# Loading q and k six tokens a partition and turning them by DMA from there, for batches 2 to 7 of an attention and MLP kernel

## The chip, the cores and the metric

The kernel runs on one core of one Trainium2 chip. The metric is the device time of one execution in microseconds; given is the median of the runs.

## What is computed

Attention with a forget gate, for 8 batches of 8 heads, 576 tokens and 64 channels a head; then an MLP over the 4,608 tokens:

```python
scores = q @ k.T / sqrt(64);  cum = cumsum(log(clip(f, 0.0001, 1)))
scores = where(causal, -1e9, scores + cum[i] - cum[j])
attn = softmax(scores);  x = attn @ v            # x: 4608 x 512, heads side by side
h = x @ w_in                                     # 512 x 2048
out = (h - tanh(h)) @ w_out                      # 2048 x 512
```

## The kernel before

**Stages.** The work goes by pairs of heads: pair p is heads 2c and 2c+1 of batch b, with p = 4b + c, so four pairs a batch and 32 in all. The loop at the end takes one pair after another; a pair's stage has seven score tiles, `ti` = 0 to 6 (`scores`). Between the tiles the loop writes, in an order fixed by hand, what else belongs to the stage: the product with v of the pair before (`values`), its division on VectorE, the turn of that result into `XR`, the MLP's input (`turn`, from batch 1 on by DMA from SP's queue), and some 6 to 8 pieces of the MLP (`mlp1`, `mlp2_plain`, `mlp2`), whose number `TAKE` sets. The MLP goes by units of 512 tokens. Every engine executes in the order of this program and waits on semaphores.

**Banks.** A score tile goes to one of two PSUM banks (`ps_sc`). The MLP takes three banks (`ps_m`) by turns and, after `widen(1)`, the bank `ps_tr` too.

**q and k.** A score matmul contracts over channels, so it needs q and k turned: channel on the partition, token along the row, in `QT` and `KT` (two buffers each, for even and odd batches), below them three rows for the decay. There are two ways to that form:

- Batches 0 to 2. `load_qk` brings a batch's heads to `qn`, `kn` with six neighbouring tokens on each of 96 partitions. `trans` turns one pair on TensorE by six transposes (two tokens by 64 channels, from 96 partitions, each), into a PSUM bank, and two copies take that to `QT` or `KT`, even tokens by one and odd tokens by the other. For batch 2 this is done in the stages of pairs 7 and 8, two pairs in each; one copy of the two is on VectorE and the other, put off by `LATER` and `rest`, on ScalarE. In these stages `keep` takes one of the three MLP banks out of turn for it; `widen(1)` comes in pair 9's stage.
- Batches 3 to 7 (`FAR` = 3). `load_block` brings 128 tokens, one a partition, in five loads for q and five for k. `turn_block` turns each block on SP's queue by a DMA transpose into `TQ` (two buffers) or `TK` (one), with two heads on the 128 partitions and the tokens in order. `place` then copies from there: k by four copies of two heads on VectorE, q by four copies of one head on ScalarE and two of two heads on VectorE.

The dictionary `LOADS` says at which pair and tile a load, a turn or a copy is written into the program; `add` fills it, batch by batch. With p0 = 4(b - 1), the first pair of the batch before, k of batch b is placed in the stages p0 + 3 and p0 + 4, its q on ScalarE in stage p0 and on VectorE in stage p0 + 1 (for batch 3 three stages later).

Of the kernel before, what the change touches and what calls it, by code (L numbers as in the profile page):

```python
# [21 lines left out]
def kernel(  # L22
# [44 lines left out]
    ps_m = ctx.enter_context(tc.tile_pool(name="ps_m", bufs=1, space=PSUM))  # L67
    M_AT, KEPT = [0], []

    def m_bank(name):  # L70
        while M_AT[0] % 3 in KEPT:
            M_AT[0] += 1
        M_AT[0] += 1
        return ps_m.tile([P, 512], FP32, tag=f"m{(M_AT[0] - 1) % 3}", name=name)

    def keep():
        while M_AT[0] % 3 in KEPT:
            M_AT[0] += 1
        KEPT.append(M_AT[0] % 3)

# [12 lines left out]
    qn, kn = ([t[0:S // NT6, :].rearrange("p (h n d) -> p h n d", h=H, n=NT6) for t in raw] for raw in (qraw, kraw))  # L93
    qb, kb = ([t[:, 0:NJ * DM].rearrange("p (n e) -> p n e", n=NJ) for t in raw] for raw in (qraw, kraw))
    vn = [qkp.tile([P, NJ, H, VW], FP16, tag=f"vn{i}", name=f"vn{i}") for i in range(2)]
# [9 lines left out]

    def load_block(dst, src, b, n):
        pn = min(P, S - n * P)
        nc.gpsimd.dma_start(out=dst[b % 2][0:pn, n, :].rearrange("p (h d) -> p h d", h=H),  # L108
                            in_=src[b, :, n * P:n * P + pn, :].rearrange("h p d -> p h d"))

    def turn_block(dst, src, b, n):
        pn = min(P, S - n * P)
        nc.sync.dma_start_transpose(out=dst[:, :, n * P:n * P + pn], in_=src[b % 2][0:pn, n, :])

    def place(dst, src, b, a, c, n, eng):
        to, of = dst[b % 2][0:D, 2 * c + a:2 * c + a + 2 * n - 1:2, 0:S], src[a * D:(a + 1) * D, c:c + n, :]
        if eng == "A":
            nc.scalar.activation(out=to, in_=of, func=AF.Copy)
        else:
            (nc.gpsimd if eng == "P" else nc.vector).tensor_copy(out=to, in_=of)  # L120

# [120 lines left out]
    for b in range(2, B):  # L242
        p0 = (b - 1) * NPAIR
        at_q = [(p0 - 2, n + 2) for n in range(NJ)]
        at_k = [(p0, n) for n in range(NJ)]
        at_v = [(p0 + (1 if b >= FAR else 2), n) for n in range(NJ)]
        to_q, to_k = (p0 - 1, 1), (p0 + 1, 4)
        on_q = p0
        on_k = (p0 + 3, 0), (p0 + 3, 2), (p0 + 4, 1), (p0 + 4, 4)
        if b == FAR:  # L250
            at_q = [(p0 - 1, n + 1) for n in range(NJ)]
            to_q, on_q = (p0, 4), p0 + 3
            on_k = (p0 + 3, 2), (p0 + 3, 4), (p0 + 4, 0), (p0 + 4, 4)
        add((p0, 0), load_aug, b)
        for n in range(NJ):
            if n < NJ - 1:
                add(at_v[n], load_v_block, b, n, 0, H)
            else:
                add(at_v[n], load_v_rest, b)
            if b < FAR:  # L260
                continue
            add(at_q[n], load_block, qb, q, b, n)
            add(at_k[n], load_block, kb, k, b, n)
            add(to_q, turn_block, TQ[b % 2], qb, b, n)
            add(to_k, turn_block, TK, kb, b, n)
        if b < FAR:
# [3 lines left out]
        for n, (c, a) in enumerate(((0, 0), (0, 1), (2, 0), (2, 1))):  # L270
            add(on_k[n], place, KT, TK, b, a, c, 2, "V")
            add((on_q, (1 if b == FAR else 3) + n), place, QT, TQ[b % 2], b, a, c // 2, 1, "A")
            if c:
                add((on_q + 1, 1 + 2 * a), place, QT, TQ[b % 2], b, a, c, 2, "V")

# [11 lines left out]
    def trans(b, c, src, dst, early, copies, split=False):  # L287
        pn, g3 = S // NT6, NT6 // 2
        if early:
            t32 = m_bank("t32")  # L290
        elif KEPT and src is kn:
            t32 = ps_m.tile([P, UW], FP32, tag=f"m{KEPT[0]}", name="t32")
        else:
            t32 = ps_tr.tile([P, UW], FP32, tag="tr", name="t32")
# [296 lines left out]
    def att_items(p):  # L591
# [8 lines left out]
        for ti in range(len(TILES)):  # L600
# [12 lines left out]
            if ti == 5 and p < NPAIR - 1:  # L613
                put(trans, *pairs[p + 2], qn, QT, True, "VV")
            if p in (2 * NPAIR - 1, 2 * NPAIR, 2 * NPAIR + 1) and (ti % 2 or ti == 0):
# [42 lines left out]
    for p in range(len(pairs) + 1):  # L658
# [17 lines left out]
        for emit, counts in items:  # L676
            emit()
            n += counts
            while n > first and given < len(mine) and given * (whole - first) < (n - first) * len(mine):
                fn, *args = mine[given]  # L680
                fn(*args)
                given += 1
    widen(2)
    for fn, *args in mlp[at:]:
# [29 lines left out]
```

## Time and profile before

| | before |
|---|---|
| median of 3 runs | 338.77 us (338.75 to 339.58) |
| profiled execution, span of its instructions | 337.1 us |
| its own time over the span | within 1.7 us, by the median of the runs |
| TensorE busy | 330.0 us (98%) |
| VectorE busy | 260.8 us (77%) |
| ScalarE busy | 233.2 us (69%) |
| GpSimd busy | 163.2 us (48%) |
| DMA packets | 147,468, of which 128,181 under 512 B |

In the rows of a profile PE is TensorE, PEld its weight loads, DVE VectorE, ACT ScalarE, POOL GpSimd, and SPq the queue of DMAs that SyncE issues. "L311 DVE COPY KT<-t 64x576 f16<-64x576 f16 x16 | 12.8, 799 | ..." is a group: line, engine, operation, written tile and read tile, shapes, count, busy time in us, mean duration in ns, and then the idle time before it. A row of the timeline begins with its start and its duration in us.

### The profile page before, as it was taken

The numbers are of one execution on the slowest core, as the hardware profiler recorded it, in microseconds if no ns is written. First come the engines' busy times: TensorE is split into PE (matmuls) and PEld (weight loads), VectorE is DVE, ScalarE is ACT, GpSimd is POOL, SyncE is SP. The second block draws the span as 40 slices with busy tenths as digits, with TensorE's granted clock in tenths as the row PEclk, the third lists the DMA queues.
The fourth block names the chain that finished last, engine by engine and source line by source line (L and its number), as shares of the span: only waits on it lengthen the run. The fifth ranks groups of instructions, "written<-read, shape, count | busy, mean of one in ns | idle before, by whom it ended". The sixth has DMA issues, their size and how long they took to land.

```text
span 337.1 us, 8726 instructions
## 1 busy us (share of the span) xinstructions
PE 330.0 (98%) x3313; PEld 235.6 (70%) x3313; DVE 260.8 (77%) x509; ACT 233.2 (69%) x438; POOL 163.2 (48%) x321
## 2 busy tenths in 40 slices
PE   8899999999999999999999999999999999999996
PEld 8775558875687558845888888656865686486485
DVE  7998986659887886778867896788668866966865
ACT  6997777978977886788677867787558733632630
POOL 8977467775667564767377637722322210000000
PEclk9999999999999999999999999999999999999999
DMA  9999999999979997999899999990130022002003
GB/s 113 143 203 202 186 198 165 184 159 172 142 87 190 136 134 72 164 152 139 94 122 187 118 112 117 163 132 18 51 113 2 19 65 97 2 31 95 0 12 116
DMA packets 147468, 38.82 MB, mean 115 GB/s; under 512 B 128181, under 2 KB 146335, under 8 KB 147426
## 3 DMA queue, kind: packets, MB, share of 16 engines
q0 software_dynamic: 94528, 18.37, 75.5%
q1 hardware_dynamic: 52892, 19.89, 32.4%
q8 instruction: 26, 0.43, 0.6%
q14 instruction: 16, 0.13, 0.2%
q10 hardware_dynamic: 6, 0.01, 0.0%
HBM read 36.85 MB, written 9.44 MB: 137 GB/s over the span
## 4 chain that ended last, share of the span: by engine, by line
PE 90%; DVE 7%; ACT 2%; issue 1%; ACTq 0%
PE hps L451 36%; PE ops L517 29%; PE ps L352 11%; PE av L389 8%; PE ops L492 4%; DVE KT L311 2%; DVE QT L311 1%; PE t L298 1%; ACT e L361 1%; DVE xn L400 1%; DVE gq L462 0%; DVE TQ L187 0%; ACT th L456 0%; PE x L417 0%; DVE clo L190 0%
## 5 line engine op out<-in xcount | busy, mean ns | idle before, releaser
L451 PE MATMUL hps<-XR,win 128*128 128x512 f16 (+1 forms) x640 | 140.7, 357 | 0.3 <-DVE gq L462 0.3
L456 ACT ACTIVATE th<-hps 128x512 f32<-128x512 f32 x144 | 86.6, 602 | 55.5 <-PE hps L451 53.5
L361 ACT ACTIVATE e<-ps 128x512 f16<-128x512 f32 x192 | 110.2, 597 | 8.9 <-PE ps L352 7.4
L462 DVE TENSOR_TENSOR gq<-hps,th 128x512 f16<-128x512 f32 x144 | 98.0, 687 | 23.6 <-ACT th L456 22.0
L371 POOL TENSOR_SCALAR_AFFINE_SELECT e<-e 128x128 f16<-128x128 f16 x168 | 60.7, 364 | 71.5 <-ACT e L361 68.7
L451 PEld LDWEIGHTS <-win 128*128 128x128 f16 x640 | 57.7, 97 | 49.0 <-issue 1.1
L352 PE MATMUL ps<-QT,KT 67*128 67x64 f16 (+4 forms) x384 | 76.5, 276 | 2.0 <-DVE KT L311 1.4
L517 PEld LDWEIGHTS <-gq 128*128 128x128 f16 x640 | 60.3, 97 | 11.1
L517 PE MATMUL ops<-wout,gq 128*128 128x256 f16 x512 | 63.2, 272 | 0.0
L352 PEld LDWEIGHTS <-KT 67*128 67x128 f16 x384 | 36.4, 98 | 23.4 <-DVE KT L311 2.0
L389 PEld LDWEIGHTS <-e 128*128 128x128 f16 x896 | 32.3, 97 | 3.6
L389 PE MATMUL av<-vn,e 128*128 128x65 f16 x896 | 33.6, 193 | 0.0
L517 PE MATMUL ops<-W,sq 128*128 128x256 f16 x256 | 31.2, 272 | 0.0
L131 POOL DMA_DIRECT2D vn<-in_v_dram x32 | 28.0, 877 | 6.5 <-DMA win<-in_moe_w_in_dram 2.9
L400 DVE TENSOR_TENSOR xn<-av,rs 128x640 f16<-128x640 f32 x32 | 26.4, 825 | 1.3 <-DVE rs L399 0.2
L517 PEld LDWEIGHTS <-sq 128*128 128x128 f16 x256 | 24.1, 97 | 3.4
L108 POOL DMA_DIRECT2D kn<-in_k_dram x25 | 21.2, 848 | 2.1 <-issue 1.8
L108 POOL DMA_DIRECT2D qn<-in_q_dram x25 | 21.2, 848 | 1.8 <-issue 1.4
L371 POOL TENSOR_SCALAR_AFFINE_SELECT el<-el 128x128 f16<-128x128 f16 x28 | 9.3, 333 | 26.1 <-ACT el L361 25.8
L398 DVE TENSOR_SCALAR rs<-av 128x10 f32<-128x10 f32 x32 | 5.2, 163 | 18.2 <-PE av L389 17.0
L532 ACT ACTIVATE m<-ops 128x512 f32<-128x512 f32 x16 | 9.5, 596 | 10.9 <-PE ops L517 10.9
L484 DVE TENSOR_TENSOR gq<-gq 128x512 f16<-128x512 f16 x32 | 17.1, 533 | 0.0
(83 smaller groups left out, 311.8 us busy)
## 6 DMA issues: line engine op xcount, KB each, us to landing
out_dram<-ost SPq DMA_DIRECT2D x34, 256.0 KB
vn<-in_v_dram POOLq DMA_DIRECT2D x24, 128.0 KB, 6.2
qn<-in_q_dram POOLq DMA_DIRECT2D x20, 128.0 KB, 5.0
kn<-in_k_dram POOLq DMA_DIRECT2D x20, 128.0 KB, 5.6
win<-in_moe_w_in_dram POOLq DMA_DIRECT2D x2, 1024.0 KB, 11.8
wout<-in_moe_w_out_dram POOLq DMA_DIRECT2D x2, 1024.0 KB, 15.6
XR<-xn SPq DMA_TRANSPOSE x56
qn<-in_q_dram POOLq DMA_DIRECT2D x6, 144.0 KB, 4.6
```

The lines of the kernel that those rows point to most:

```text
L108: nc.gpsimd.dma_start(out=dst[b % 2][0:pn, n, :].rearrange("p (h d) -> p h d", h=H), in_=src[b, :, n * P:n * P + pn, :].rearrange("h p d - ...
L131: nc.gpsimd.dma_start(out=vn[b % 2][:, n, h0:h1, 0:D], in_=v[b, h0:h1, n * P:(n + 1) * P, :].rearrange("h p d -> p h d"))
L352: nc.tensor.matmul(out=ps[:, col:col + n], lhsT=kt[0:rows, h, j * P:(j + 1) * P], rhs=qt[0:rows, h, i0:i0 + n], start=True, stop=cut == 0)
L361: nc.scalar.activation(out=e[:, lo:hi], in_=ps[:, lo:hi], func=AF.Exp, bias=-SHIFT, scale=qscale)
L371: nc.gpsimd.affine_select(out=view, in_=view, compare_op=ALU.is_ge, fill=0.0, base=0, pattern=pat, channel_multiplier=-1)
L389: nc.tensor.matmul(out=av[:, a, ib, :], lhsT=E.pop((b, c, a, j, ib)), rhs=vn[b % 2][:, j, 2 * c + a, 0:D + 1], start=(j == 0), stop=(j == ib))
L400: nc.vector.tensor_tensor(out=xn.rearrange("p i (a d) -> p a i d", a=2), in0=av[:, :, :, 0:D], in1=rs.to_broadcast([P, 2, NJ, D]), op=ALU. ...
L451: nc.tensor.matmul(out=hps[:, o:o + n], lhsT=win[:, ci, ft * P:(ft + 1) * P], rhs=XR[:, ci, t:t + n], start=(ci == 0), stop=(ci == NCH - 1))
L456: nc.scalar.activation(out=th, in_=hps, func=AF.Tanh, scale=-1.0)
L462: nc.vector.tensor_tensor(out=GQ[(u, i)][:, half, kt, :], in0=hps, in1=th, op=ALU.add)
L484: nc.vector.tensor_tensor(out=LHS[name](u, i)[:, ks], in0=LHS[x](u, i)[:, ks], in1=LHS[y](u, i)[:, ks], op=op)
L517: nc.tensor.matmul(out=ps[:, m, :], lhsT=LHS[lhs](u, kt // 4)[:, kt % 4, m * P:(m + 1) * P], rhs=rhs[:, kt, :], start=(fresh and (apart or ...
```

## The change

q and k of batches 3 to 7 are loaded by `load_qk`, as those of batches 0 to 2 were: one DMA with six tokens a partition in place of five. `turn_raw` turns four heads of such a buffer by one DMA transpose, so two for q and two for k: 12 blocks of 128 by 96, each with two tokens by 64 channels on its partitions and one row of 96 token groups. So `TQ` and `TK` now hold, for a head, three such blocks, and even tokens lie on partitions 0 to 63, odd ones on 64 to 127. `place` copies one parity of four heads (on ScalarE of two): it reads tokens at a step of 96 elements and writes them at a step of 2.

Batch 2 goes this way too. Its loads stay in pair 4's stage; it is turned in pair 6's stage and placed by eight copies on VectorE in those of pairs 7 and 8. TensorE's transposes for it, their copies and `keep` are gone, and `widen(1)` comes in pair 7's stage. v of batch 2 is loaded in pair 7's stage in place of pair 6's. For batch 3, q is loaded, turned and placed in other stages than before; for batches 4 to 7 the loads stand at one tile.

```diff
-    def load_block(dst, src, b, n):
-    ...
-    def turn_block(dst, src, b, n):
-        pn = min(P, S - n * P)
-        nc.sync.dma_start_transpose(out=dst[:, :, n * P:n * P + pn], in_=src[b % 2][0:pn, n, :])
-
-    def place(dst, src, b, a, c, n, eng):
-        to, of = dst[b % 2][0:D, 2 * c + a:2 * c + a + 2 * n - 1:2, 0:S], src[a * D:(a + 1) * D, c:c + n, :]
+    def blocks(t):
+        return t.rearrange("p c (g r) -> p (c g) r", r=S // NT6)
+
+    def turn_raw(dst, src, b, h0, h1):
+        nc.sync.dma_start_transpose(out=blocks(dst)[:, 3 * h0:3 * h1, :],
+                                    in_=src[b % 2][0:S // NT6, h0 * NT6 * D:h1 * NT6 * D])
+
+    def place(dst, src, b, h0, h1, e, eng):
+        to = dst[b % 2][0:D, h0:h1, e:S:2].rearrange("d h (r g) -> d h r g", g=NT6 // 2)
+        of = blocks(src)[e * D:(e + 1) * D, 3 * h0:3 * h1, :].rearrange("d (h g) r -> d h r g", g=NT6 // 2)
...
     for b in range(2, B):
         p0 = (b - 1) * NPAIR
-        at_v = [(p0 + (1 if b >= FAR else 2), n) for n in range(NJ)]
+        late_b = b >= FAR
+        at_v = [(p0 + (1 if late_b else 3), n) for n in range(NJ)]
...
+        if not late_b:
             add((p0, 2), load_qk, qn, q, b, 0, H)
             add((p0, 5), load_qk, kn, k, b, 0, H)
+            for n in range(2):
+                add((p0 + 2, 1 + 3 * n), turn_raw, TQ[0], qraw, b, 4 * n, 4 * n + 4)
+                add((p0 + 2, 2 + 3 * n), turn_raw, TK, kraw, b, 4 * n, 4 * n + 4)
+                for e in range(2):
+                    add((p0 + 3 + n, 1 + e), place, QT, TQ[0], b, 4 * n, 4 * n + 4, e, "V")
+                    add((p0 + 3 + n, 4 + e), place, KT, TK, b, 4 * n, 4 * n + 4, e, "V")
             continue
...
+        at_q, at_k, to_q, to_k = (p0 - 2, 2), (p0, 1), (p0 - 1, 1), (p0 + 1, 4)
+        on_q = p0
+        on_k = (p0 + 3, 0), (p0 + 3, 2), (p0 + 4, 1), (p0 + 4, 4)
+        if b == FAR:
+            at_q, at_k, to_q, to_k = (p0, 1), (p0, 5), (p0 + 1, 4), (p0 + 2, 4)
+            on_q = p0 + 3
+            on_k = (p0 + 3, 2), (p0 + 3, 4), (p0 + 4, 0), (p0 + 4, 4)
+        add(at_q, load_qk, qn, q, b, 0, H)
+        add(at_k, load_qk, kn, k, b, 0, H)
+        for n in range(2):
+            add(to_q, turn_raw, TQ[b % 2], qraw, b, 4 * n, 4 * n + 4)
+            add(to_k, turn_raw, TK, kraw, b, 4 * n, 4 * n + 4)
+        for n in range(4):
+            m, e = divmod(n, 2)
+            add(on_k[n], place, KT, TK, b, 4 * m, 4 * m + 4, e, "V")
+            add((on_q, (1 if b == FAR else 3) + n), place, QT, TQ[b % 2], b, 2 * m, 2 * m + 2, e, "A")
+            if m:
+                add((on_q + 1, 1 + 2 * e), place, QT, TQ[b % 2], b, 4, H, e, "V")
...
-            if p in (2 * NPAIR - 1, 2 * NPAIR) and ti % 2 == 0:
-                pair = pairs[2 * NPAIR + 2 * (p - 2 * NPAIR + 1) + ti // 4]
-                put(trans, *pair, *((kn, KT) if ti % 4 else (qn, QT)), False, "VA")
...
         if p == 2 * NPAIR - 1:
-            keep()
-        if p == 2 * NPAIR + 1:
-            KEPT.clear()
             widen(1)
```

The order in which SP issues its DMAs in the stages of pairs 6 and 7. Before (XR is the turned result of a pair, out_dram an output of the MLP):

```order
L423 DMA_TRANSPOSE XR<-xn 128x4x128
L425 DMA_TRANSPOSE XR<-xn 128x64
L423 DMA_TRANSPOSE XR<-xn 128x4x128
L425 DMA_TRANSPOSE XR<-xn 128x64
L499 DMA out_dram<-ost 128x2x256
L423 DMA_TRANSPOSE XR<-xn 128x4x128
L425 DMA_TRANSPOSE XR<-xn 128x64
L499 DMA out_dram<-ost 128x2x256
```

The same place now:

```order
L417 DMA_TRANSPOSE XR<-xn 128x4x128
L419 DMA_TRANSPOSE XR<-xn 128x64
L102 DMA_TRANSPOSE TQ_107<-qn_97 128x12x96
L102 DMA_TRANSPOSE TK<-kn_99 128x12x96
L417 DMA_TRANSPOSE XR<-xn 128x4x128
L419 DMA_TRANSPOSE XR<-xn 128x64
L102 DMA_TRANSPOSE TQ_107<-qn_97 128x12x96
L102 DMA_TRANSPOSE TK<-kn_99 128x12x96
L493 DMA out_dram<-ost 128x2x256
L417 DMA_TRANSPOSE XR<-xn 128x4x128
L419 DMA_TRANSPOSE XR<-xn 128x64
```

Two turns of batch 2 stand ahead of the turns of pair 5's result, and two more behind them.

VectorE in the stages of pairs 7 and 8 (t is a bank with TensorE's transposes, rs and xn are the division of a pair's result, W a difference of output weights). Before:

```order
L462 TENSOR_TENSOR gq<-hps,th 128x512 x2
L311 COPY QT_103<-t_1152 64x576
L311 COPY KT_105<-t_1183 64x2x288
L398 TENSOR_SCALAR rs<-av 128x10
L399 RECIPROCAL rs<-rs 128x10
L400 TENSOR_TENSOR xn<-av,rs 128x2x5x64
L311 COPY QT_103<-t_1270 64x576
L311 COPY KT_105<-t_1300 64x2x288
L311 COPY QT_103<-t_1329 64x576
L278 TENSOR_TENSOR W_93<-wout 128x1024
L311 COPY KT_105<-t_1362 64x2x288
```

Now:

```order
L456 TENSOR_TENSOR gq<-hps,th 128x512 x2
L111 COPY QT_103<-TQ_107 64x1152 x2
L392 TENSOR_SCALAR rs<-av 128x10
L393 RECIPROCAL rs<-rs 128x10
L394 TENSOR_TENSOR xn<-av,rs 128x2x5x64
L111 COPY KT_105<-TK 64x4x288 x2
L111 COPY QT_103<-TQ_107 64x1152
L274 TENSOR_TENSOR W_93<-wout 128x1024
L111 COPY QT_103<-TQ_107 64x1152
```

Each copy of a pair from PSUM has become half of a copy of two pairs from `TQ` or `TK`, and the copies of pairs 8 and 9 into KT stand ahead of those of pairs 10 and 11 into QT. In the later stages the copies `place` stand where they stood, with another pattern.

More of the change, by code (lines that the diff above doesn't have):

```diff
@@ L67 @@
     ps_m = ctx.enter_context(tc.tile_pool(name="ps_m", bufs=1, space=PSUM))
-    M_AT, KEPT = [0], []
+    M_AT = [0]
     def m_bank(name):
-        while M_AT[0] % 3 in KEPT:
-            M_AT[0] += 1
         M_AT[0] += 1
         return ps_m.tile([P, 512], FP32, tag=f"m{(M_AT[0] - 1) % 3}", name=name)
[L76 to L79, printed above, removed]
     win = wpl.tile([P, NCH, DFF], FP16)
@@ L119, in place @@
         else:
-            (nc.gpsimd if eng == "P" else nc.vector).tensor_copy(out=to, in_=of)
+            nc.vector.tensor_copy(out=to, in_=of)
     def load_v_rest(b):
```

30 lines of the change are left out of this document (2 added, 28 removed).

## Prediction

> **What bounds the kernel now.** I read the page first, then its chain, then the busy time of each engine in the stages around the change, then single rows of the timeline, the groups by form and the DMA queues. A "stage" here is the stretch from the first score matmul of one pair of heads to the first of the next; stage 7 is pair 7's.
>
> ```profile
> span 337.1 us, 8726 instructions
> PE 330.0 (98%) x3313; PEld 235.6 (70%) x3313; DVE 260.8 (77%) x509; ACT 233.2 (69%) x438; POOL 163.2 (48%) x321
> PE 90%; DVE 7%; ACT 2%; issue 1%; ACTq 0%
> ```
>
> TensorE is busy for 98% of the span and holds 90% of the chain that ended last: its work sets the time. So a thing counts only if it takes matmuls off TensorE, or makes TensorE wait where it did not wait before.
>
> ```profile
> 50.75:59.31 8.56, 8.55 (x114) 7.47 (x114) 5.16 (x9) 6.44 (x11) 6.58 (x14) 1.00 2.04 163
> 86.50:95.00 8.50, 8.50 (x88) 6.08 (x87) 7.49 (x16) 8.40 (x17) 4.32 (x10) 1.00 1.90 131
> 95.00:103.40 8.40, 8.40 (x99) 7.21 (x98) 7.44 (x17) 5.96 (x12) 6.85 (x13) 1.00 0.94 100
> 148.14:156.50 8.36, 8.36 (x72) 4.49 (x70) 7.10 (x14) 7.03 (x15) 4.76 (x11) 1.00 1.84 141
> 156.50:165.74 9.24, 9.24 (x92) 6.44 (x90) 8.03 (x19) 6.52 (x14) 4.53 (x11) 1.00 1.26 116
> 165.74:174.16 8.42, 8.42 (x100) 7.22 (x99) 5.39 (x13) 6.08 (x12) 6.83 (x13) 1.00 0.92 93
> 174.16:183.55 9.39, 9.39 (x109) 8.02 (x107) 6.74 (x13) 6.86 (x14) 6.25 (x12) 1.00 1.81 185
> ```
>
> The rows are stages 7, 11, 12 and 18 to 21; after the length come PE, PEld, DVE, ACT and POOL, then the clock (1.00 throughout). TensorE fills every stage. VectorE has 8.03 of 9.24 us in stage 19 and leaves between 1.2 and 3.0 us in the stages around it; ScalarE has 8.40 of 8.50 us in stage 11.
>
> **Term 1: the turns of batch 2 leave TensorE.** Eight groups of six transposes (4 pairs, q and k) are in stages 7 and 8.
>
> ```profile
> 59.22 0.26 PE t L298 x6
> 59.47 0.22 PE ps L352
> L298 PE MATMUL t<-id,qn 96*128 96x96 f16 x72 | 5.0, 206 | 0.0
> ```
>
> The first two rows are of the chain in order of time: a group takes 0.26 us of TensorE's sequence. The third, 5.0 us for 72, would give 0.42 a group, but it counts the tail of the last transpose, under which the next matmul already runs. I take 8 x 0.26 = **2.1 us less**. Nothing else waits in its place by itself: TensorE had no idle time there to give back.
>
> **Term 2: what batch 2 now waits for.** q and k of batch 2 are loaded as before; now SP's queue must turn them once they land, and VectorE must place them before stage 8's first score. Before, TensorE turned them just ahead of use.
>
> ```profile
> qn<-in_q_dram POOLq DMA_DIRECT2D x1, 576.0 KB, 14.6
> kn<-in_k_dram POOLq DMA_DIRECT2D x1, 576.0 KB, 16.1
> 32.27 0.79 POOL L102 DMA_DIRECT2D qn<-in_q_dram  x1
> 33.80 0.78 POOL L102 DMA_DIRECT2D kn<-in_k_dram  x1
> 39.83 1.50 SPq L423 DMA_TRANSPOSE XR<-xn  x1
> 59.31 0.38 PE L352 MATMUL ps<-QT,KT 67*128 67x512 f16 x1
> ```
>
> q lands at 32.27 + 14.6 = 46.9, k at 33.80 + 16.1 = 49.9. Stage 8 begins at 59.31; four of the eight groups stand before it, so it would begin at 59.31 - 4 x 0.26 = 58.3. Between 46.9 and 58.3 must fit: the turn of q's first half, behind it in the same queue that of k's first half, and two copies on VectorE. How long a turn takes at that time is seen from the turn issued at 39.83, in the DMA rows of 40 to 43.5, 43.5 to 47.5 and 53 to 58 us:
>
> ```profile
> q0 software_dynamic: 1132, 0.69, 137.1%
> q8 instruction: 1, 0.02, 1.6%
> ...
> q0 software_dynamic: 834, 0.63, 100.2%
> q1 hardware_dynamic: 640, 0.15, 29.8%
> ...
> q0 software_dynamic: 3894, 0.61, 169.6%
> q1 hardware_dynamic: 591, 0.14, 30.2%
> ```
>
> Turns are in queue q1. None of its packets ran up to 43.5, some 4 us after the issue; then the 640 of one pair's turns took most of 4 us, beside the loads. Half of q (4 heads) is twice a pair's two heads, so 1,280 packets. At 640 in 4 us they would take 8 us; the load beside them is then the second half of the output weights, in smaller packets, that ends at about 53, so I take 5: 46.9 + 4 + 5 = 56. k's half follows at once, beside v's small packets, where both queues together pass (3894 + 591) / 5 = 900 packets a us; with half of that, 1280 / 450 = 2.8 us, it lands at 58.7. Two copies (0.79 each, below) end at 60.3, against 58.3: TensorE waits **2.0 us**. Bounds: if the 4 us to the first packet run while q's half is under way and k's half goes at 900 a us, it lands at 49.9 + 4 + 1.4 = 55.3, and there is no wait; at 8 us for q's half it lands at 61.7 and the wait is 5.0 us. I take the middle because the packets beside it are between those of the two rows. Behind the copies on VectorE stand the division of pair 6 and the differences of the weights, for which TensorE has a stage of time. On SP's queue pair 5's, 6's and 7's turns into XR now stand behind those of batch 2; pair 7's is wanted first for unit 1 of the MLP:
>
> ```profile
> 66.97 1.23 SPq L425 DMA_TRANSPOSE XR<-xn  x1
> 72.23 1.03 PE L451 MATMUL hps<-XR,win 128*128 128x512 f16 x4
> ```
>
> It had 5.3 us from issue to use, and the turn issued at 39.83 needed up to 7.7 (its packets ended by 47.5). I take **0.3 us**, from 0 (the stage is itself later) to 1.
>
> **Term 3: VectorE's copies get a broken source.** Batches 3 to 7: 20 copies for K and 10 for Q, 64x1152, now read at a step of 96 elements and written at a step of 2, as the copies after TensorE's turns always were. No such copy from SBUF is in the trace; its neighbours:
>
> ```profile
> L311 DVE COPY QT<-t 64x576 f16<-64x576 f16 x18 | 14.4, 800 | 2.2 <-PE t L298 2.1
> L120 DVE COPY KT<-TK 64x1152 f16<-64x1152 f16 x20 | 9.4, 470 | 0.3
> L311 DVE COPY KT<-t 64x288 f16<-64x288 f16 x4 | 1.9, 477 | 0.1
> L419 DVE COPY XR<-x 128x576 f16<-128x576 f16 x2 | 0.9, 456 | 0.6 <-PE x L417 0.5
> ```
>
> From PSUM the broken pattern costs 800 for 576 elements, 477 for 288: 1.12 ns an element on 154 ns. The unbroken one, 456 for 576, is (456 - 154) / 576 = 0.52: breaking the runs doubles the price of an element. From SBUF unbroken it is (470 - 154) / 1152 = 0.27; doubled, 0.55, and 0.55 x 1152 + 154 = 790 ns. That is my value; the bounds are 470 (no loss) and 1.12 x 1152 + 154 = 1,444 ns (PSUM's price).
>
> Added: 30 x 0.32 = 9.6 us of VectorE, at most two copies a stage, so 0.64: stage 19 goes from 8.03 to 8.67 of 9.24 us, stage 20 from 5.39 to 6.03 of 8.42. The idle time there covers it; the sums behind a copy come 0.3 us later and the banks are asked for again later than that. I take **0.2 us** for all, from 0 to 1. Batch 2's eight copies replace eight of 0.80 on VectorE and eight on ScalarE: no cost but in term 2.
>
> **Term 4: ScalarE's copies.**
>
> ```profile
> L118 ACT ACTIVATE QT<-TQ 64x576 f16<-64x576 f16 x20 | 13.7, 683 | 0.5
> L309 ACT ACTIVATE QT<-t 64x576 f16<-64x576 f16 x4 | 3.3, 817 | 0.1
> ```
>
> At most 683 to 817, 0.13 each, four in a stage: 0.5 us. In stage 11 ScalarE has 0.1 us left, so up to 0.4 us of delay pass into stage 12, which has 2.4. **0.2 us**, from 0 to 0.5.
>
> **What costs nothing.** Five loads of 848 ns become one for each of q and k: some 35 us less on POOL and fewer, longer packets.
>
> ```profile
> L108 POOL DMA_DIRECT2D qn<-in_q_dram x25 | 21.2, 848 | 1.8 <-issue 1.4
> PEld L352 <- DVE KT L311: 2.0, 3, 1.1
> PE ps L352 <- DVE KT L311: 1.4, 2, 0.9
> ```
>
> The waits of TensorE that the view lists at all are for copies into KT (the last two rows), none for POOL or a load; so nothing is gained, and nothing lost: if POOL were late with its masks, they would be wanted a stage later. v of batch 2, a stage later, is issued from about 52 and wanted in stage 9, after 70. SP issues four turns a batch in place of ten.
>
> **Sum.** -2.1 + 2.0 + 0.3 + 0.2 + 0.2 = +0.6 us. The profiled execution spans 337.1, the median is 338.8, 1.7 more; a difference carries over: 337.7 of span, **339.4 us**. A measurement of this kernel can tell some 0.3%, 1.0 us, so this is just within no change.
>
> **Rivals.**
> *A, no wait at stage 8* (the turns land by 56.7). Then -2.1 + 0.4 = -1.7: 337.0 us; with no cost for the copies, 336.7. For it: 11.4 us lie between q's landing and stage 8, and the turn issued at 39.83 had passed by 47.5. Against: two turns, each twice as long, in one queue, and k lands only at 49.9.
> *B, the broken copies cost PSUM's price*, 1.44 us. At stage 8 the two copies end 1.3 later: 3.3 of wait. In stages 19 to 21 each pair of copies adds 1.95: stage 19 wants 9.98 of 9.24, 0.74 passes on into stage 20, 5.39 + 1.95 + 0.74 = 8.08 of 8.42. VectorE then runs without a pause for two stages; TensorE waits where more than the banks' reserve queues up, which I put at 0.4 us a batch, 2.0 in five. Sum: -2.1 + 3.3 + 0.3 + 2.0 + 0.2 = +3.7: 342.5 us. It decides from 8.03 + 2 x (price - 0.47) > 9.24, a price of 1.08 us. For it: the only broken copies in the trace pay it. Against: the doubling, which the unbroken ones bear out. [...]
>
> **How the numbers follow.** Forecast 0.52 (its own range 337.2 to 342.4, from term 2's bounds), A 0.25, B 0.15; 0.08 for a copy dearer than B's or a jam on SP's queue. Faster by over 1.0 us: A and a little of the forecast, 0.28. Within: half of the forecast, 0.25. Slower: the other half, B and the rest, 0.47. The range runs from A's 336.7 to B's 342.5.
>
> **What would show it.** Right: in stages 7 and 8 no L298 rows and the stages' own work 1.0 us shorter each; before stage 8's first score a wait of TensorE for a copy into KT of about 2 us, and that copy released by a DMA; copies from TK at about 0.79 us; stages 18 to 21 within 0.1 us of before. Wrong: no such wait (A), copies above 1.1 us with stages 19 and 20 longer (B), a wait for XR at unit 1 of more than 1 us, or a stage after 12 that TensorE does not fill.

## The result, and the profile after

The changed kernel takes **347.74 us** (median of 4 runs, 346.51 to 349.35) against 338.77: 1.026 times as long, 95% interval 1.023 to 1.029. The forecast was 339.4 us with a range up to 342.5; it is slower by more than any case that was priced. The profiled execution spans 346.0 us; with the same 1.7 us around the span as before that is the median.

The head of the page of the changed kernel, and the shares of its chain of waits by engine:

```profile
span 346.0 us, 8491 instructions
PE 331.7 (96%) x3265; PEld 234.9 (68%) x3265; DVE 270.0 (78%) x509; ACT 229.2 (66%) x430; POOL 135.3 (39%) x281
PE 75%; DMA 11%; POOL 6%; DVE 3%; ACT 2%; issue 1%; ACTq 0%
```

TensorE's share of the chain fell from 90% to 75%, and DMA, which had none, has 11%. GpSimd's busy time fell by 28 us, where some 35 were foretold, and brought nothing. Where the time went is seen by stages. Rows of the busy time by stretches (length, then PE, PEld, DVE, ACT, POOL, then the clock): stage 7, the wait at its end in two pieces, stage 8 in two pieces, and stage 11.

```profile
50.77:63.53 12.76, 7.69 (x91) 6.38 (x90) 5.96 (x10) 4.83 (x9) 7.55 (x14) 0.93 1.78 146
58.47:61.86 3.39, 0.00 (x0) 0.00 (x0) 2.58 (x6) 0.60 (x1) 1.00 (x1) 1.00 2.39 126
61.86:63.53 1.67, 0.00 (x1) 0.01 (x1) 1.60 (x2) 0.00 (x0) 0.00 (x0) 0.50 2.34 147
63.53:68.69 5.16, 5.16 (x30) 3.56 (x31) 1.84 (x3) 1.87 (x4) 1.79 (x3) 0.50 1.49 171
68.69:73.57 4.88, 4.88 (x64) 4.25 (x62) 4.38 (x8) 2.37 (x5) 2.13 (x3) 1.00 1.19 213
92.05:102.10 10.05, 8.54 (x89) 5.98 (x86) 8.63 (x18) 9.74 (x18) 3.39 (x9) 1.00 1.14 166
```

Stage 7 grew from 8.56 to 12.76 us though its own work shrank to 7.69; stage 8 from 8.73 to 10.04, half of it (5.16 us) at half clock; stage 11 from 8.49 to 10.05. Stages 13, 17, 21 and 25 grew by 0.34 each. These are 4.20 + 1.31 + 1.56 + 1.36 = 8.4 of the 8.9 us; the rest lies in stages that grew by 0.1 or less and in the work after the last pair's first score, and was not followed.

The wait ahead of stage 8, in rows of the timeline: SP's queue, then VectorE, then TensorE (start, duration, and in brackets the idle time before, with what ended it).

```profile
46.97 1.61 SPq L102 DMA_TRANSPOSE TQ<-qn  x1
50.02 3.52 SPq L102 DMA_TRANSPOSE TK<-kn  x1
...
57.16 2.77 SPq L102 DMA_TRANSPOSE TQ<-qn  x1
60.02 4.51 SPq L102 DMA_TRANSPOSE TK<-kn  x1
```

```profile
58.35 1.62 DVE L111 COPY QT<-TQ 64x1152 f16<-64x1152 f16 x2 [5.92 <-DMA TQ<-qn]
...
61.86 1.61 DVE L111 COPY KT<-TK 64x1152 f16<-64x1152 f16 x2 [0.73 <-DMA TK<-kn]
```

```profile
63.53 0.61 PE L346 MATMUL ps<-QT,KT 67*128 67x512 f16 x1 [5.06 <-DVE KT L111]
```

q's first turn was issued at 46.97 and landed at 58.33, k's was issued at 50.02 and landed at 61.83: 11.4 and 11.8 us. VectorE stood 5.92 us for the first. Then came the two copies for q and the division of pair 6; VectorE then stood another 0.73 us for k's turn, so that landing, and not the copies and the division before it, set the end of the wait here. After the two copies for k TensorE had waited 5.06 us. SP's issues, 1.2 us each for a turn before, became 1.6 to 4.5 us for batch 2's.

How the turns' packets pass is seen in the DMA queues, here from 51 to 55 us and then from 56 to 57 (queue, kind: packets, MB, share); q0 is the load of the output weights' second half, q1 the turns:

```profile
q0 software_dynamic: 958, 0.49, 88.3%
q1 hardware_dynamic: 948, 0.24, 45.9%
...
q1 hardware_dynamic: 85, 0.02, 62.9%
q0 software_dynamic: 28, 0.01, 35.2%
```

In the first stretch the two queues pass packets nearly one for one: 958 and 948 in 4 us, some 237 a us each.

At 237 a us the 1,152 packets of q's first half (96 x 1536 elements of 2 bytes, 256 bytes a packet: 0.24 MB in the 948) take 4.9 us. From 51 to 56 us 1,366 packets passed in q1, more than these, and q's turn still landed only at 58.33. From 56 to 57 us all queues together passed 113 packets, where they had passed 476 a us. What held them then, no run shows.

### The profile page after: what moved, and what is told of

Same layout as the page of the kernel before. It is cut to its first block, busy times and chain, and to the rows that moved or that the text cites. A ratio compares the mean times of both kernels' runs of the same rounds, so it can differ in the third digit from the quotient of the medians.

```text
span 346.0 us, 8491 instructions
## 1 busy us (share of the span) xinstructions
PE 331.7 (96%) x3265; PEld 234.9 (68%) x3265; DVE 270.0 (78%) x509; ACT 229.2 (66%) x430; POOL 135.3 (39%) x281
## 4 chain that ended last, share of the span: by engine, by line
PE 75%; DMA 11%; POOL 6%; DVE 3%; ACT 2%; issue 1%; ACTq 0%
PE hps L445 31%; PE ops L511 25%; PE ps L346 9%; DMA kn<-in_k_dram 8%; PE av L383 6%; DMA TK<-kn 3%; PE ops L486 3%; POOL qn L94 2%; ACT e L355 1%; POOL vn L122 1%; POOL kn L94 1%; DVE KT L111 1%; DVE gq L456 1%; ACT QT L109 1%; DVE sq L478 1%
## 5 line engine op out<-in xcount | busy, mean ns | idle before, releaser
L365 POOL TENSOR_SCALAR_AFFINE_SELECT e<-e 128x128 f16<-128x128 f16 x168 | 65.0, 390 | 101.6 <-ACT e L355 98.8
L346 PE MATMUL ps<-QT,KT 67*128 67x64 f16 (+4 forms) x384 | 77.3, 279 | 9.0 <-DVE KT L111 6.6
L511 PE MATMUL ops<-wout,gq 128*128 128x256 f16 x512 | 63.2, 272 | 0.0
L346 PEld LDWEIGHTS <-KT 67*128 67x128 f16 x384 | 37.1, 98 | 32.1 <-DVE KT L111 7.1
L365 POOL TENSOR_SCALAR_AFFINE_SELECT el<-el 128x128 f16<-128x128 f16 x28 | 10.1, 359 | 34.6 <-ACT el L355 34.3
L111 DVE COPY KT<-TK 64x1152 f16<-64x1152 f16 x24 | 20.2, 842 | 1.1 <-DMA TK<-kn 0.7
L111 DVE COPY QT<-TQ 64x1152 f16<-64x1152 f16 x14 | 11.6, 826 | 9.5 <-DMA TQ<-qn 9.3
L486 PE MATMUL ops<-wout,gq 128*128 128x256 f16 x128 | 18.1, 291 | 0.0
L109 ACT ACTIVATE QT<-TQ 64x576 f16<-64x576 f16 x20 | 17.1, 855 | 0.5
```

Source lines behind the costliest of these rows:

```text
L111: nc.vector.tensor_copy(out=to, in_=of)
L346: nc.tensor.matmul(out=ps[:, col:col + n], lhsT=kt[0:rows, h, j * P:(j + 1) * P], rhs=qt[0:rows, h, i0:i0 + n], start=True, stop=cut == 0)
L365: nc.gpsimd.affine_select(out=view, in_=view, compare_op=ALU.is_ge, fill=0.0, base=0, pattern=pat, channel_multiplier=-1)
L486: nc.tensor.matmul(out=ops[:, m, :], lhsT=GQ[(u, ft % NK // 4)][:, half, ft % 4, t0:t0 + P], rhs=wout[:, ft, e * HE:(e + 1) * HE], start=( ...
L511: nc.tensor.matmul(out=ps[:, m, :], lhsT=LHS[lhs](u, kt // 4)[:, kt % 4, m * P:(m + 1) * P], rhs=rhs[:, kt, :], start=(fresh and (apart or ...
```

## The experiments

Lengths of stages (us) in the profiled execution of each kernel, its span, and the median time with the range of its runs. Where the runs of one kernel differ by several us, its profile is one of them.

| kernel | 7 | 8 | 9 | 11 | 12 | 13 | span | time |
|---|---|---|---|---|---|---|---|---|
| before | 8.56 | 8.73 | 9.26 | 8.49 | 8.40 | 9.35 | 337.1 | 338.8 |
| changed | 12.76 | 10.04 | 9.26 | 10.05 | 8.44 | 9.69 | 346.0 | 347.7 (346.5 to 349.4) |
| b2_tensor | 8.56 | 8.73 | 9.26 | 10.15 | 8.44 | 9.68 | 340.6 | 346.3 (342.3 to 347.8) |
| b3_blocks | 13.53 | 9.51 | 10.39 | 8.49 | 8.40 | 9.67 | 344.9 | 346.4 (345.0 to 347.4) |
| early | 8.27 | 7.56 | 17.44 | 10.02 | 8.44 | 9.68 | 349.3 | 350.9 (346.0 to 351.5) |
| warm | 12.00 | 7.55 | 16.34 | 10.03 | 8.44 | 9.68 | 350.3 | 352.3 (352.1 to 353.1) |
| v_later | 12.32 | 10.02 | 9.26 | 12.02 | 11.12 | 9.69 | 350.3 | 348.9 (347.6 to 352.0) |
| early_tail | 10.01 | 7.56 | 14.76 | 10.02 | 8.44 | 9.68 | 347.0 | 348.8 (347.3 to 350.1) |
| q_spread | 8.56 | 8.72 | 9.26 | 10.12 | 8.44 | 9.26 | 339.3 | 341.0 (340.7 to 346.7) |
| k_pair | 8.56 | 8.73 | 9.26 | 8.38 | 8.45 | 9.50 | 337.5 | 340.6 (339.2 to 343.1) |
| k_early | 8.55 | 8.72 | 9.26 | 8.38 | 8.45 | 10.96 | 339.0 | 339.7 (339.2 to 342.4) |
| hybrid | 8.56 | 7.55 | 12.73 | 8.50 | 12.09 | 11.81 | 346.9 | 343.7 (342.9 to 348.6) |
| half_dma | 8.55 | 7.55 | 13.32 | 8.38 | 8.45 | 9.45 | 340.4 | 341.0 (340.1 to 342.2) |
| aug_later | 8.56 | 7.55 | 9.26 | 10.03 | 8.44 | 10.62 | 339.4 | 339.0 (338.3 to 341.2) |
| kn_later | 8.56 | 7.55 | 9.26 | 12.87 | 11.37 | 9.26 | 343.6 | 344.0 (342.6 to 345.4) |
| both_later | 8.56 | 7.55 | 9.26 | 8.38 | 8.45 | 10.52 | 337.6 | 343.0 (338.5 to 345.8) |
| v_spread | 8.56 | 7.55 | 9.26 | 8.38 | 8.45 | 9.38 | 336.4 | 338.3 (338.2 to 338.7) |
| v_spread_k | 8.55 | 7.55 | 9.26 | 8.38 | 8.46 | 9.38 | 336.5 | 338.4 (338.1 to 340.4) |

### The two halves of the change

*b2_tensor*: batch 2 on TensorE as before (its transposes, `keep`, v in pair 6's stage), batches 3 to 7 the new way.

> The new loads, turns and copies for batches 3 to 7, but batch 2 turned on TensorE and its v loaded as before the change. Theory (arrival): no wait at stage 8, 2.1 us of transposes back; left is what the copies cost, 1.5 us in stage 11 and 0.3 us in four later stages: 338.8 + 3 = 341.5 us. Rival (copies carry the loss): 345 us or more.

*b3_blocks*: batch 2 the new way, batches 3 to 7 with `load_block`, `turn_block` and the old `place`.

> Batch 2 the new way, but batches 3 to 7 loaded, turned and copied in blocks as before the change. Theory (arrival): the wait at stage 8 and the half clock stay, the copies' cost goes: 338.8 - 2.1 + 5.1 + 2.4 = 344 us, or more if the small packets of batch 3's loads delay the turns further. Rival (copies): 338 to 340 us.

In the profiles the halves part cleanly: without batch 2's turns stages 7 to 9 are as before, to 0.01 us, and what is left is stage 11 and the four stages with 0.34; with blocks from batch 3 on, stage 11 is 8.49 and stage 17 9.35, and stages 7 to 9 are 6.9 us longer (stage 13, 9.67 here too, was not followed). So each stall belongs to one half. But the times don't follow the profiles: b2_tensor's four runs lie between 342.3 and 347.8 us, the profiled one being the shortest. So its profile fits its theory (341.5 us), and its median of 346.3 the rival's 345 and more. Something more comes and goes with the new way from batch 3 on; it comes back below.

### The wait and the clock at stage 8

*early*: batch 2's loads ahead of the output weights.

```diff
-            add((p0, 2), load_qk, qn, q, b, 0, H)
-            add((p0, 5), load_qk, kn, k, b, 0, H)
+            add((p0 - 1, 4), load_qk, qn, q, b, 0, H)
+            add((p0 - 1, 5), load_qk, kn, k, b, 0, H)
```

> The changed kernel with one edit: q and k of batch 2 are loaded in pair 3's stage, ahead of the output weights in the DMA queue, in place of pair 4's. Theory (arrival): the loss is TensorE's 5.1 us wait for the late turn of batch 2 and the half clock behind that wait (some 2.4 us), so both go: 347.7 - 7.5 = 340 us; what is left over is 1.5 us in stage 11 and 0.3 us in each of stages 13, 17, 21, 25. Rival (copies): the dearer copies on VectorE and ScalarE carry the loss and the early load changes little: 345 us or more.

*warm*: 80 matmuls of 128 columns into the two score banks, read by none, ahead of stage 8's first score.

> The changed kernel with 80 matmuls of 128 columns, read by none, written into the two score banks ahead of stage 8's first score, so that TensorE works through most of its wait. Theory (clock): the wait for batch 2's K stays as long, but the granted clock stays at 1.0 behind it and stage 8 falls from 10.0 to 7.6 us: 345.3 us. Rival: stage 8 is long for another reason (late DMAs): 347 us or more.

Rows by stretches of warm, stages 8 and 9:

```profile
63.27:70.82 7.55, 7.55 (x93) 6.46 (x91) 2.35 (x5) 4.24 (x8) 2.46 (x6) 1.00 1.63 162
70.82:87.16 16.34, 12.04 (x88) 6.67 (x87) 9.07 (x15) 6.46 (x13) 8.38 (x13) 0.79 1.58 191
```

The clock part is shown: with TensorE kept busy through the wait, stage 8 takes 7.55 us in place of 10.04. So 2.5 us of the loss are the clock after the wait, not the wait. In the trace of the changed kernel TensorE is idle from 58.47, and the clock is 0.50 from 61.86, 3.4 us later; it is 1.00 again from 68.69, after 5.2 us of work.

In early the wait ahead of stage 8 fell to 0.6 us and stage 8 to 7.56, nearly as its theory had it. But both kernels lost elsewhere what they had won, and more. Rows of early, stages 6 and 9, and the waits of TensorE there:

```profile
42.32:52.91 10.59, 8.31 (x82) 4.98 (x82) 9.25 (x16) 6.58 (x13) 2.57 (x8) 1.00 1.38 187
...
68.74:86.19 17.45, 12.12 (x89) 6.84 (x87) 8.34 (x14) 6.46 (x13) 8.32 (x13) 0.80 1.55 175
```

```profile
PEld L486 <- DMA wout<-in_moe_w_out_dram: 2.5, 1, 2.5
```

```profile
PE hps L445 <- DMA XR<-xn: 3.7, 1, 3.7
```

With batch 2's loads ahead of them in early, the output weights came 2.5 us late. And stage 9 grew by 8 us in early and 7 in warm, which neither expectation had: the MLP waited for pair 7's turn into XR, and TensorE's clock fell again (0.80 in early and 0.79 in warm, as the mean of the stage). In both kernels the chain runs through VectorE, which stood for q's second turn (issued at 53.82 in early, landed 11.7 us later) ahead of the division of pair 7, and then through the turn into XR itself, 9.8 us in early.

*early_tail* tests VectorE's part: early, with the copies for pairs 10 and 11 behind that division, at the last two tiles of stage 8.

> The kernel with batch 2's q and k loaded ahead of the output weights, and in addition the copies for pairs 10 and 11 at the last two tiles of stage 8, behind the division of pair 7, in place of its first ones. Theory (VectorE, in order, waits for the second Q turn and so the division of pair 7, its turn into XR and the MLP's input come late; TensorE starves in stage 9): stage 9 falls from 17.44 us to about 9.5, the division ends some 5 us earlier, span about 341 and time about 343 us. Rival (the turn into XR is late by itself, behind batch 2's turns and batch 3's loads, 8 to 10 us each): stage 9 stays above 14 us, 348 to 351 us.

The division ended at 66.3 in place of 69.0, and stage 9 still took 14.76 us: the theory that VectorE's order makes the stall held for 2.7 of its 8 us, and the rest fits the rival. (Stage 7 is 1.7 us longer than in early; this was not followed.) The turn into XR was issued at 68.63, 2.3 us after the division, and landed 9.07 us later. The chain in order of time (start, duration):

```profile
67.21 0.64 SPq L191
...
67.90 0.62 SPq L191
...
68.63 9.07 DMA XR<-xn
```

Ahead of it on SP's queue stood the decay rows (L191).

*v_later* tests whether v's packets are what slows the turns: batch 2's v at the last two tiles of stage 7 and the first two of stage 8.

> The changed kernel, with v of batch 2 issued behind the turns, at the last two tiles of stage 7 and the first two of stage 8. Theory (the turn's packets take turns one for one with those of whatever load runs beside them, and beside v's small packets K's first turn gets about 200 to 300 packets a us where it had 435 to 560 almost alone): K's first turn lands some 2.5 us earlier, TensorE's wait ahead of stage 8 falls from 5.06 to about 2.5 us, too short for the clock to fall, and stage 8 is about 7.6 us: span about 341, time about 343 us. Rival (the turn is slow by itself): same wait of 5 us, half clock behind it, 347 to 348 us.

For "too short for the clock to fall" there was one wait at hand: 2.3 us in stage 6 of early, with the clock at 1.00. Without v's packets the turns' pass faster, as the theory has it. From 58 to 60 us, with almost nothing beside it, the turns' queue passes 834 packets a us, where in the changed kernel it had 237 beside the weights and, in the same 2 us, 241 beside v (483 against 832, so not one for one):

```profile
q1 hardware_dynamic: 1667, 0.40, 133.3%
q0 software_dynamic: 7, 0.00, 1.0%
```

k's turn landed 2.3 us earlier (59.55), the second ones 5 us earlier. Yet TensorE's wait stayed at 4.6 us, and stage 8 at 10.02. The chain says why:

```profile
47.15 11.36 DMA TQ<-qn
...
60.75 0.49 DVE xn L394
...
61.49 0.79 DVE KT L111
```

q's first turn, beside the weights, was as slow as ever, and between it and k's copies on VectorE stand q's copies and the division. So v's packets do not set this wait: once k's turn lands in time, q's turn and VectorE's order do. That it is the weights' packets that make q's turn slow is likely, but no run took them away with all else as it was. The same profile has a stall that the changed kernel's lacks: batch 3's first K turn landed only at 98.94, 7.3 us into stage 11 (in the changed kernel 3.7), and stages 11 and 12 are 12.02 and 11.12.

### Stage 11 and the stages with 0.34

*q_spread*: on b2_tensor, ScalarE's Q copies at other tiles.

```diff
-            add((on_q, (1 if b == FAR else 3) + n), place, QT, ...
+            at = (on_q + n // 2, 1 + n % 2) if b == FAR else (on_q + 3 * (n // 2), 4 + 2 * (n % 2) - 2 * (n // 2)) if b == FAR + 1 else (on_q, 1 + n)
+            add(at, place, QT, ...
```

> The kernel with batch 2 on TensorE and the new way from batch 3 on, with ScalarE's Q copies at other tiles: for batch 3 two in stage 11 and two in stage 12 in place of four in stage 11, for batch 4 two in stage 12 and two in stage 15, for batches 5 to 7 two tiles earlier. Theory (ScalarE has too little room where these copies stand, 0.855 us each in place of 0.683): stage 11 back from 10.15 to about 8.6, stages 13, 17, 21 and 25 from 9.68 to about 9.35: span 340.6 - 1.6 - 1.3 = 337.7, time 339.5 us where nothing else comes. Rival (the added time is not of ScalarE but of the copies into KT on VectorE or of the turns): stages as they were, span 340 to 341. On the scatter of that kernel's runs (342 to 348): if it hangs on ScalarE's load it goes, otherwise it stays, up to 345.

Half right. Stages 13 and 25 are 9.26 us (below the 9.35 of before), stage 21 9.30: there it was ScalarE's copies where they stood. The chain of the changed kernel shows how, here in stage 17: it leaves TensorE and runs through such a copy and the reading of the scores on either side of it.

```profile
147.04 0.56 ACT e L355
147.63 0.46 ACT QT L109
...
148.97 0.38 PE ps L346 x2
```

Stage 15, which got two of the copies, rose from 9.24 to 9.47. Stage 17 is 9.50 in this profile, behind a turn into XR of 7.75 us, and 9.26 in k_pair with the same copies. Stage 11 stayed at 10.12, with ScalarE at 8.49 us in place of the changed kernel's 9.74: that theory fell.

*k_pair*: on q_spread, batch 3's first two K copies side by side.

```diff
-            on_k = (p0 + 3, 2), (p0 + 3, 4), (p0 + 4, 0), (p0 + 4, 4)
+            on_k = (p0 + 3, 2), (p0 + 3, 2), (p0 + 4, 0), (p0 + 4, 4)
```

> The kernel with ScalarE's Q copies spread, where stage 11 stayed at 10.12 us, and one more edit: the two copies that bring heads 0 to 3 of batch 3's K stand side by side at the third tile of stage 11, in place of the third and the fifth. Theory (a copy of one parity leaves every head half done, so stage 12's first score waits for the second copy too, which stood behind the division and five products on VectorE and ended at 96.76; a copy of whole heads, as before the change, let head 0 go with the first copy at 92.3): the second copy ends near 93.9, before TensorE wants it at about 95.2, stage 11 is 8.5 to 8.6 us, span 339.3 - 1.6 = 337.7, time 339.4 us. Rival (VectorE has too little room in stages 10 and 11 with the dearer copies, wherever they stand): stage 11 stays above 9.5 us, or stage 12 takes over what it loses; 341 us.

The copies into KT on VectorE in stage 11 of the kernel before, where stage 12 began at 95.02:

```profile
91.83 0.44 DVE L120 COPY KT<-TK 64x1152 f16<-64x1152 f16 x1
...
95.24 0.46 DVE L120 COPY KT<-TK 64x1152 f16<-64x1152 f16 x1
```

The end of stage 11 in the chain of the changed kernel, in order of time:

```profile
97.56 0.74 DVE KT L111
...
98.63 0.82 DVE xn L394
99.45 1.76 DVE sq L478 x5
...
101.23 0.82 DVE KT L111
...
102.10 0.39 PE ps L346
```

and k_pair's copies on VectorE and its stage 11:

```profile
92.02 1.63 DVE L118 COPY KT<-TK 64x1152 f16<-64x1152 f16 x2
```

```profile
86.58:94.95 8.37, 8.37 (x88) 6.04 (x86) 6.96 (x13) 7.43 (x15) 2.75 (x8) 1.00 1.20 192
```

Stage 11 falls by 1.74 us to 8.38, below the kernel before. The cause is shown: the old copy brought whole heads, so head 0 was ready with the first, and stage 12's first score ran before the second copy had begun; the new one brings one parity of four heads, so a score needs both, and the second stood behind the division and five products. The order of VectorE's instructions had not changed; what its rows mean had. The runs still lie between 339.2 and 343.1.

### Half of batch 2 by DMA, and the stall of stage 9

*hybrid*: the kernel before with pairs 10 and 11 alone turned by DMA. *half_dma*: the same on k_pair.

> The kernel before, with pairs 10 and 11 of batch 2 alone turned by DMA (one turn for q issued at the sixth tile of stage 6, one for k at the second of stage 7) and placed by four copies of VectorE at the last four tiles of stage 8; pairs 8 and 9 on TensorE as before, batches 3 to 7 in blocks as before. Theory (the turns need 10 to 12 us beside the loads, which they have here: 49 to 61 and 54 to 66 us, and no copy that waits stands ahead of a division): stage 8 gives back four groups of transposes, 4 x 0.26 = 1.05 us: 337.7 us. Rival (the two turns delay those of pairs 5 to 7 into XR on the one queue, and the MLP waits in stages 8 or 9): 1 to 8 us more, 339.5 to 346 us.

> As the kernel with K's two copies side by side, with pairs 10 and 11 of batch 2 turned by DMA as well (q at the sixth tile of stage 6, k at the second of stage 7, four copies on VectorE at the last tiles of stage 8). Theory (half of batch 2's turns, with batch 3's loads as one DMA each, leave XR's turns at 4 to 6 us, and stage 8 loses four groups of transposes, 1.0 us): span 336.7, time 338.4 us. Rival (XR's turns stretch to 8 us and more again, as they did where batch 3 was loaded in blocks, and the MLP waits in stage 9): 1 to 4 us more, 340 to 343 us.

Stage 8 gives back 1.18 us in both, as expected, and stage 9 takes 3.5 to 4.1: the rivals. hybrid's profiled run is its longest and stalls in stages 12 and 13 too. *aug_later* and *kn_later* take one suspect each out of the way of pair 7's turn into XR in half_dma, *both_later* both.

```diff
-        add((p0, 0), load_aug, b)
+        add((p0, 4 if b == FAR else 0), load_aug, b)      # aug_later
-            at_q, at_k, to_q, to_k = (p0, 1), (p0, 5), (p0 + 1, 4), (p0 + 2, 4)
+            at_q, at_k, to_q, to_k = (p0, 1), (p0 + 1, 3), (p0 + 1, 4), (p0 + 2, 4)      # kn_later
```

> As the kernel with half of batch 2 turned by DMA, and batch 3's three decay rows written behind pair 7's turns into XR on SP's queue (fifth tile of stage 8 in place of its first). Theory (SP's queue, in order, is what makes pair 7's XR late: its result was divided at 64.1 us, but its first turn was issued only at 67.05, behind an issue of 4.9 us for batch 2's K turn and 2.1 us for the decay rows, and landed at 74): the turn is issued 1 to 2 us earlier and lands by 72, stage 9 falls from 13.3 to 10.5 to 11.5 us, span about 338, time 339 to 340 us. Rival (it is late by the packets of batch 3's k load beside it): issued earlier, lands as late, stage 9 above 12.5 us, 341 us.

> As the kernel with half of batch 2 turned by DMA, and batch 3's k loaded behind pair 7's turns into XR (fourth tile of stage 9 in place of the sixth of stage 8). Theory of SP's queue: turn still issued near 67, stage 9 above 12 us, 341 us. Rival (packets of 768 B that take turns with those of XR, 120 to 200 a us of each beside one another against 400 and more without them): the turns of pair 7 pass in 3 to 4 us in place of 7, stage 9 is about 10 us, span about 337.2, time 339 us.

> Both edits together. Whichever of the two delays pair 7's XR is gone: stage 9 about 9.3 to 9.6 us, stage 8 7.55; span 336.7, time 338.4 us, the first of these that is level with or below the kernel before. If stage 9 stays above 11 us, neither is the cause, and the turns themselves are slow to start; 340 us.

SP's queue in half_dma, in aug_later and in kn_later:

```profile
55.31 4.86 SPq L109 DMA_TRANSPOSE TK<-kn  x1
...
64.91 0.68 SPq L198 DMA_DIRECT2D KT<-chi  x1
65.64 0.63 SPq L198 DMA_DIRECT2D KT<-clo  x1
66.33 0.62 SPq L198 DMA_DIRECT2D QT<-chi  x1
67.05 1.22 SPq L426 DMA_TRANSPOSE XR<-xn  x1
```

```profile
65.62 1.91 SPq L426 DMA_TRANSPOSE XR<-xn  x1
```

```profile
67.32 1.22 SPq L426 DMA_TRANSPOSE XR<-xn  x1
```

Stage 9 is 9.26 us in aug_later, kn_later and both_later, against 13.32 in half_dma. In aug_later, issued 1.4 us earlier, the turn landed at 71.6 in place of 74.06; in kn_later, issued as late but without k's load beside it, it passed in 3.9 us in place of 7.0 and landed at 71.2. So both theories hold: late issue and shared packets add up to the wait, and taking away either is enough. kn_later then pays for its k load: batch 3's K turn landed at 96.5 and stages 11 and 12 grew by 7.4 us together. both_later missed: its profile spans 337.6 us, but six of its ten runs took 342.7 to 345.8.

### The rest of the scatter

*k_early*: on k_pair, batch 3's K turns at the second tile of stage 10.

> As the kernel with K's two copies side by side, and batch 3's K turned at the second tile of stage 10 in place of the fifth, ahead of the turns of pair 9 into XR. Theory (the scatter between runs comes from the landing of batch 3's K turn, which in the profiles so far came 4 to 7 us after stage 11's start with a copy asked for at 5.5): the profile reads as that kernel's, 337.7 us of span, and all runs lie within 1 us, at 339 to 340 us. Rival (the scatter is of other transfers, XR's above all, which now stand behind two more turns): some runs still 3 to 6 us longer, or stages 10 and 11 longer by 1 us and more.

*v_spread*: on aug_later, VectorE's copies of stages 12 and 13 spread over 12, 13 and 16. *v_spread_k*: that with k_early's edit.

```diff
-            on_k = (p0 + 3, 2), (p0 + 3, 2), (p0 + 4, 0), (p0 + 4, 4)
+            on_k = (p0 + 3, 2), (p0 + 3, 2), (p0 + 4, 5), (p0 + 5, 1)
-                add((on_q + 1, 1 + 2 * e), place, QT, ...
+                add((on_q + 1 + e, 3 - e) if b == FAR else (on_q + (4 if b == FAR + 1 else 1), 1 + 2 * e), place, QT, ...
```

> As the kernel with the decay rows written later (half of batch 2 by DMA), with VectorE's copies of stages 12 and 13 spread: of batch 3's second half two copies in stage 12 and two in 13 in place of four in stage 12, and batch 4's two Q copies in stage 16 in place of 13. Theory (four copies of 0.82 us in stage 12 overload VectorE, which ran without a pause from 93.7 to 107 us and held the MLP's output bank, 1.4 to 1.7 us in stage 13): stage 13 falls from 10.6 to about 9.4, the rest of the scatter is batch 3's K turn in stage 11: span 336.5 where that turn is in time, 338 where not; median 338.3, some runs to 340. Rival (VectorE is late only because it waits for the turn, so that stage 13 follows stage 11): stage 13 as long as before wherever stage 11 is 10 us, runs 338.3 to 341 as before.

> The same, and batch 3's K turned at the second tile of stage 10, ahead of pair 9's turns into XR. Theory (K's landing was the last wait that differs from run to run): stages 11 and 13 at 8.4 and 9.4 us in every run, 338.0 to 338.5 us, below the kernel before (338.8). Rival (pair 9's XR, now behind the two turns, is late for the MLP in stages 11 to 13): runs up to 342 us again.

k_early missed: stage 13 grew to 10.96 and its nine runs lie between 339.2 and 342.4. v_spread hit: its eleven runs lie within 0.6 us, at 338.30 us, 0.9984 times the kernel before (0.9976 to 0.9993), so just below the kernel before (0.5 us). The rival, that stage 13 only follows stage 11, is settled by both_later and k_early: stage 11 is 8.38 us in all three, stage 13 10.5 to 11.0 in those two and 9.38 here. v_spread's span, and stages 8, 9 and 13:

```profile
span 336.4 us, 8537 instructions
```

```profile
59.32:66.87 7.55, 7.55 (x94) 6.47 (x92) 5.28 (x9) 5.79 (x11) 3.61 (x7) 1.00 1.42 156
66.87:76.13 9.26, 9.26 (x88) 6.07 (x86) 7.15 (x12) 6.46 (x13) 8.29 (x13) 1.00 1.34 222
...
102.19:111.57 9.38, 9.38 (x88) 6.05 (x86) 8.46 (x15) 6.43 (x13) 7.62 (x12) 1.00 1.41 180
```

Turning K earlier on top of that did not help (338.39, one run at 340.4). What stays open: the copies that v_spread moves come after batch 3's K turn, which landed 2.4 us earlier in its profile than in aug_later's; why it was in time in all eleven runs is not shown, nor what the 5 to 7 us were by which the runs of b2_tensor and of both_later differ, since the profiles are of short runs.

## Why the prediction was wrong

**Term 1 was right.** Stages 7 and 8 of the changed kernel hold 2.0 us less work (8.56 to 7.69, and 8.73 to the 7.55 of warm), against 2.1.

**Term 2 failed, in size.** The place and the mechanism were as written, a wait of TensorE for a copy into KT that a DMA released, but it was 5.06 us, just past the upper bound of 5.0, in place of 2.0. The step that failed is the time of the two turns. q's half was given 4 us to its first packet and 5 for its packets, to land at 56; it landed at 58.33, 11.4 us after its issue. k's half was to follow 2.8 us behind and followed 3.5 behind. Those 2.4 + 0.7 us are the 3.1 that were missing. The rate was not the error: 237 packets a us make 4.9 us, as the 5 had it. The time between the packets and the landing had no term, and its cause stays open but for the stretch from 56 to 57 us in which the queues hardly moved. q's copies and a division, which the sum left out too, cost nothing here, since k's turn landed behind them; in v_later they set the wait.

**The clock was no term at all.** The forecast had it at 1.00 throughout and put nothing for what a wait does to it. The wait of 5 us cost 2.5 us more at half clock, in stage 8, shown by warm. Terms 1, 2 and the clock make 5.06 + 2.5 - 2.0 = 5.5 us; stages 7 and 8 grew by 5.51.

**Term 3 had the price right and the meaning wrong.**

```profile
L111 DVE COPY KT<-TK 64x1152 f16<-64x1152 f16 x24 | 20.2, 842 | 1.1 <-DMA TK<-kn 0.7
L111 DVE COPY QT<-TQ 64x1152 f16<-64x1152 f16 x14 | 11.6, 826 | 9.5 <-DMA TQ<-qn 9.3
L109 ACT ACTIVATE QT<-TQ 64x576 f16<-64x576 f16 x20 | 17.1, 855 | 0.5
```

These are the groups by form of the changed kernel, with mean ns of one. VectorE's copies take 826 to 842 ns against 790 foretold and 470 before: rival B's 1,444 is refuted, and stage 19 is 9.24 us as it was. So the broken pattern cost a copy into KT 0.37 us here (842 ns against 470), which does not reach PSUM's price; whether the step of the reads or that of the writes costs it, no run parts. But 0.2 us for all stages missed stage 11, 1.56 us, because a copy of a parity finishes no head (k_pair).

**Term 4 failed, in size.** ScalarE's copies take 855, above the bound of 817. The term looked at stage 11 alone, but four of them in one stage cost 0.34 us in each of stages 13, 17, 21 and 25, 1.4 in all against 0.2 (q_spread took it away in stages 13, 21 and 25). Stage 21 was to stay within 0.1 us of before; 18 to 20 did.

**The turns behind batch 2's** got 0.3 us. The changed kernel's own profile has no such wait: TensorE's wait and half clock at stage 8 gave them the time, it seems, for without the one (early) or the other (warm) they cost 7 to 8 us in stage 9. **What costs nothing** held as far as the runs show: GpSimd has 30 us less work in b2_tensor too, and none of its stages 7 to 25 is shorter than before.

Of the rivals, A (no wait) and B (the price) were both wrong; the loss was term 2's and that of things without a term.

## What to carry over

Price a DMA by the packets that run beside it on the other queue (948 against 958 in 4 us beside the weights here), leave room between its packets and its landing (4.9 us at that rate, 11.4 from issue to landing), and count what its issue holds up behind it (4.9 us in half_dma); a wait of TensorE as long as the eight of 3.5 us or more in these profiles is to be priced with a half clock behind it, 2.5 us behind the 5.06 of the changed kernel. When a copy's shape changes, ask which consumer's first tile is whole after the first copy: an unchanged order of instructions can hide a changed dependence. Where removing a wait makes another appear (stage 8, then 9, then 11), the transfers as a whole are late, and fewer of them at that time is the cure to try: here half of batch 2 by DMA gave 1.2 us in stage 8 and could be kept, where all of it cost 5.5 us in stages 7 and 8.

## What the runs showed of the hardware that was not expected

- Beside the load of the weights batch 2's turns got as many packets as the load, some 237 a us each (948 against 958 in 4 us); beside v 241 against 416 (changed kernel, 58 to 60 us), and almost alone 834 (v_later). They took 9.0 to 11.8 us from issue to landing in the changed kernel; those of the kernel before, which are smaller, 6.4 to 7.6 where issued between 39 and 60 us and 2.3 to 6.4 between 65 and 108.
- A turn's issue, 1.2 us on SP in most of the kernel before, took 4.5 to 4.9 us for batch 2's K turns with several turns under way (4.51 in the changed kernel, 4.78 in aug_later, 4.86 in half_dma), and what stood behind it on the queue was issued only after it (the next DMA at 64.63 in the changed kernel, behind an issue that began at 60.02).
- ScalarE's copy with a broken pattern on both sides took 855 ns for 64x576, more than the 817 of the copy of that size from PSUM.
- In the profiles here eight single waits of TensorE were of 3.5 us or more: 3.5 and 4.6 in v_later, 3.7 in early and in early_tail, 4.1 in warm, 4.3 in kn_later, 5.1 in the changed kernel and 5.8 in b3_blocks. In the changed kernel, early and warm the clock then stood at 0.50 for 6.8 us; over the whole of the profiled execution the mean granted clock was 0.981 in v_later, with its two waits, 0.995 in early_tail and 0.99 in the other five. Shorter waits went both ways. With 2.2 us in half_dma the clock fell (0.87 as the mean of the 13.32 us of stage 9). With 2.3 us in stage 6 of early and 1.5 us in stage 11 of aug_later it stayed at 1.00, and behind 2.3 us ahead of stage 8 in early_tail the first score took 0.39 us, against 0.61 at half clock in the changed kernel. hybrid, whose longest single wait of TensorE listed from 45 to 105 us is 1.8 us, has a mean of 0.99. In half_dma and early_tail a mean of 0.995 over the whole makes some 3.5 us of half clock.
